# Attention with parallel feed-forward: shifted exponential readings summed in pairs by an accumulating DMA, and the normalisation on GpSimd

## The chip, the cores and the metric

One NeuronCore of one Trainium2 chip runs the whole program. The metric is the device time of one execution in microseconds (us). Each number for a kernel is the median of several executions.

## The reference

The kernel computes a layer norm of x (2048 rows of 640), multi-query attention with 32 heads of 20 columns and one shared key and value head, a feed-forward of 1728 columns with SiLU beside it, and the sum of both with x.

```
xn = layernorm(x)                                   # x: (1, 2048, 640) bf16
q  = (xn @ wq) as 32 heads of 20;  k = xn @ wk;  v = xn @ wv      # k, v: 2048 x 20
scores = q k^T / sqrt(20);  p = softmax(scores);  o = p v
out = x + (o as 2048 x 640) @ wo + silu(xn @ w1) @ w2
```

## The kernel before

**Blocks.** Scores are computed transposed, in blocks of 128 keys by 512 queries of one head: 32 heads x 4 query chunks x 16 key tiles = 2048 blocks (NB). Four heads of one query chunk form a group of 64 blocks (GB), so there are 32 groups (NG). A score step (do_S, matmuls at L1127) takes three or four blocks at once, each with a contraction of 20 rows in its own quarter of the array, into one PSUM bank per block.

**Two ways to an exponential.** Of a step's blocks, most are taken by ScalarE: one activation over two or three banks writes exp(scores) as bf16 into the ring E (L1161). The others (chosen in pick_dve) are taken by VectorE (L1176). The queries are scaled beforehand so that a score is in units of 1/128 of a power of two; adding OFF and writing the result as a 16-bit integer gives bits which, read as bf16, are a piecewise linear approximation of the exponential. This is a reading of the block, in a buffer Z that holds three blocks (a triple). To cancel the error of the approximation, GpSimd adds two constants to the bits (flush_z, L1202, as 64-bit integer adds over a whole triple), which gives two shifted readings in a buffer Y. The three readings of a block, with shifts 0, 43 and 86 and weights 1, 0.8046875 and 0.625 (PH), are all multiplied with V, and the three products are summed in PSUM. The weights are in V: self.v holds three copies of it, each scaled by its weight. A block of ScalarE uses copy 0 alone.

**PV.** The PV matmuls (do_pv, L968) take V as weights, 32 columns wide, four heads in the four quarters of the array, and accumulate over all keys in one PSUM bank per group. A 21st column of V holds half of the weight and gives the row sums of the softmax. A block of ScalarE is one such matmul, a block of VectorE is three.

**After a group** its bank is copied to U (L1245), transposed by a DMA issued on SP (L1216), and normalised on VectorE: a reciprocal of the sums (L1231) and one multiply (L1236), into o. When all heads of a query chunk are there, o is transposed by DMA (try_oT) and the output matmuls (out_job) follow.

**Other work on TensorE** is cut into jobs and laid between the score steps: the query projections (qd_job, whose results are copied to their places in qT by small DMAs on SP, L1303), the first feed-forward matmul (h_job, with a tanh on ScalarE, L1336, and a multiply on VectorE, L1341) and the second with the output projection (out_job, results at L1405, L1412, L1424).

**Order.** The order of every engine's instructions is made while the program is built. A planner (class Sched and Builder.step) runs a model of the five engines in which each instruction has a duration and a priority. It commits instructions one after the other, and the program is these five lists with semaphore waits between them, so on the chip no engine changes its order. The model's numbers (durations, the time after which a DMA's result counts as there, thresholds for choices) therefore set what stands behind what. 29 thresholds (28 before the change) are given anew for each 32 blocks, in a table SEG of 64 rows. Those that matter here: TILE_CAP is the number of VectorE blocks that a head may have (in self.nz), DVE_TH and DVE_TH2 the planned backlog of VectorE up to which a step gives it a first and a second block. NZ, NY and NBLK are the numbers of Z buffers, Y buffers and blocks in E.

Of the kernel before, what the change touches and what calls it, by code (L numbers as in the profile page):

```python
# [8 lines left out]
BF16 = mybir.dt.bfloat16  # L9
# [5 lines left out]
ALU = mybir.AluOpType  # L15

P = 128
# [18 lines left out]
UT_LATE = 2.0  # L36
UT_LATE1 = 4.0
# [8 lines left out]
PH = ((0, 1.0), (43, 0.8046875), (86, 0.625))  # L46
# [4 lines left out]
NBLK = 35  # L51
NZ = 8
NY = 4
# [51 lines left out]
YP_FIX = 0.147  # L105
YP_BLK = 0.218
# [13 lines left out]
            "ACT4", "SPLIT", "U2", "LOOK", "W4", "M3")  # L120
SEG = (
# [105 lines left out]
class Sched:  # L227
# [81 lines left out]
    def commit(self, op, start):  # L309
        e = op.eng  # L310
        if op.on_pick is not None:
            op.on_pick(op)
# [130 lines left out]
def t_dve_ps(n):  # L443
    return n / 960.0 + 0.067
# [1438 lines left out]
```

## Time and profile before

| | |
|---|---|
| median of 3 runs | 669.36 us (669.29 to 669.47) |
| profiled execution | 669.12 us, of which 667.3 us from the first to the last instruction (the span) |
| granted TensorE clock | 1.00 throughout |
| TensorE busy | 659.4 us |
| ScalarE busy | 647.7 us |
| VectorE busy | 601.3 us |
| GpSimd busy | 404.6 us |

The span has three parts. In the first 18.5 us the rows of x are loaded, their statistics taken and the first projections made. From 18.5 us, where the first exponential starts, to about 654 us ScalarE takes one exponential after the other while TensorE, VectorE and GpSimd work beside it. The last 13 us are the last group's normalisation and the last output matmuls. In the views below PE is TensorE's array, PEld its weight port, DVE VectorE, ACT ScalarE, POOL GpSimd and SP the engine that issues most DMAs; L with a number is a line of the kernel. Instructions that issue a DMA do not count as busy. A matmul's duration includes its way through the array, so the next begins before its end. A row of a wait names the engine and line that waited, what ended the wait, the total, the number of waits and the longest one.

### The profile page before, as it was taken

The page shows a single profiled execution, that of the slowest core. Times are in us where ns is not written, and L with a number is a line of the kernel's source. Part 1 is how long each engine was busy: PE and PEld are TensorE (multiplying, and loading weights), DVE is VectorE, ACT ScalarE, POOL GpSimd, SP SyncE. Part 2 cuts the span into 40 slices and gives each one's busy share as a digit, 9 for nine tenths or more (in the row PEclk, how much of TensorE's full clock was granted, in tenths as well). Part 3 has the DMA queues.
Part 4 walks back from the last instruction along what each step waited for, and adds up shares of the span by engine and source line. Part 5 has one row for each costly group of instructions (what it writes and reads, how often), then busy time and mean ns, then how long its engine had stood idle before and what let it go on. Part 6 is the DMA issues. An engine that isn't in the chain of part 4 may idle for free.

```text
span 667.3 us, 22800 instructions
## 1 busy us (share of the span) xinstructions
PE 659.4 (99%) x9735; PEld 220.4 (33%) x9735; DVE 601.3 (90%) x1085; ACT 647.7 (97%) x737; POOL 404.6 (61%) x509
## 2 busy tenths in 40 slices
PE   8999999999999999999999999999999999999998
PEld 4432233332323322233333323233233333223345
DVE  7888999999989999999889999988999999998783
ACT  7999999999999999999999999999999999999993
POOL 2056457777486656676556653866767674676550
PEclk9999999999999999999999999999999999999999
DMA  7565201010012210000003110000002121001001
GB/s 211 110 213 150 73 14 12 2 26 2 18 44 62 57 10 17 3 10 18 19 10 84 41 32 17 10 10 18 10 13 47 38 57 37 10 10 31 5 11 41
DMA packets 51433, 26.73 MB, mean 40 GB/s; under 512 B 38566, under 2 KB 50694, under 8 KB 51334
## 3 DMA queue, kind: packets, MB, share of 16 engines
q1 hardware_dynamic: 51190, 25.12, 14.5%
q8 instruction: 78, 1.28, 0.8%
q14 instruction: 21, 0.17, 0.1%
q10 hardware_dynamic: 144, 0.16, 0.1%
HBM read 11.44 MB, written 2.62 MB: 21 GB/s over the span
## 4 chain that ended last, share of the span: by engine, by line
PE 87%; ACT 7%; DVE 3%; SPq 1%; DMA 1%; issue 0%; ACTq 0%
PE psall L968 33%; PE psall L1127 28%; PE psall L870 26%; ACT sbt L1161 6%; DVE sbt L1176 2%; ACT sbt L1336 1%; SPq L1531 1%; DMA sbt<-in_A_x_dram 1%; DVE sbt L1424 0%; PE psall L1326 0%; DVE sbt L1236 0%; ACT sbt L1620 0%; DVE sbt L1666 0%; DVE sbt L1771 0%; ACT sbt L1655 0%
## 5 line engine op out<-in xcount | busy, mean ns | idle before, releaser
L1161 ACT ACTIVATE sbt<-psall 128x1024 bf16<-128x1024 f32 (+2 forms) x649 | 620.1, 1129 | 3.5 <-PE psall L1127 2.6
L1202 POOL INT64_ADD sbt<-sbt x492 | 399.7, 827 | 244.4 <-DVE sbt L1176 171.3
L1176 DVE TENSOR_SCALAR sbt<-psall 128x512 uint16<-128x512 f32 x732 | 473.1, 683 | 46.3 <-PE psall L1127 37.1
L968 PE MATMUL psall<-sbt 128*32 128x512 bf16 x3512 | 265.0, 383 | 0.2
L1127 PE MATMUL psall<-sbt 32*128 32x512 bf16 x2048 | 245.8, 384 | 2.1 <-ACT sbt L1161 0.7
L870 PE MATMUL psall<-sbt 128*32 128x320 bf16 (+2 forms) x3923 | 220.7, 331 | 0.5 <-DVE sbt L1176 0.4
L1127 PEld LDWEIGHTS psall<-sbt 32*128 32x128 bf16 x2048 | 61.9, 91 | 241.4 <-ACT sbt L1161 161.1
L870 PEld LDWEIGHTS psall<-sbt 128*32 128x32 bf16 x3923 | 84.6, 95 | 84.6 <-issue 54.4
L968 PEld LDWEIGHTS psall<-sbt 128*32 128x32 bf16 x3512 | 64.4, 95 | 101.3 <-issue 64.6
L1336 ACT ACTIVATE sbt<-psall 128x512 bf16<-128x512 f32 x54 | 39.6, 739 | 0.0
L1341 DVE SCALAR_TENSOR_TENSOR sbt<-sbt,psall 128x512 bf16<-128x512 bf16 x54 | 36.6, 682 | 2.6 <-ACT sbt L1336 1.2
L1245 DVE CAST sbt<-psall 128x512 bf16<-128x512 f32 x32 | 21.8, 681 | 5.4 <-PE psall L968 5.3
L1236 DVE TENSOR_TENSOR sbt<-sbt 128x320 bf16<-128x320 bf16 x31 | 18.3, 591 | 0.1
L846 PE MATMUL psall<-sbt 128*128 128x512 bf16 (+4 forms) x55 | 15.2, 428 | 1.2 <-DVE sbt L1590 1.2
L1424 DVE SCALAR_TENSOR_TENSOR sbt<-psall,sbt 128x320 bf16<-128x320 f32 x28 | 13.1, 477 | 2.9 <-PE psall L870 2.9
L1405 DVE SCALAR_TENSOR_TENSOR sbt<-psall,sbt 128x320 bf16<-128x320 f32 x28 | 13.5, 483 | 1.6 <-PE psall L870 1.4
L1294 DVE TENSOR_SCALAR sbt<-psall 128x512 bf16<-128x512 f32 (+1 forms) x19 | 12.9, 680 | 0.1
L1635 DVE BATCH_NORM_STATS2 sbt<-sbt 128x6 f32<-128x320 bf16 x22 | 10.0, 470 | 0.9 <-DMA sbt<-in_A_x_dram 0.7
L1421 ACT ACTIVATE sbt<-psall 128x320 bf16<-128x320 f32 x4 | 1.7, 438 | 8.7 <-PE psall L870 8.7
L846 PEld LDWEIGHTS psall<-sbt 128*128 128x128 bf16 x55 | 5.5, 109 | 9.1 <-issue 4.0
L1231 DVE RECIPROCAL sbt<-sbt 128x16 f32<-128x16 bf16 x31 | 7.5, 243 | 0.0
L1620 ACT ACTIVATE sbt<-sbt 128x640 bf16<-128x640 bf16 x5 | 3.6, 730 | 3.2 <-DMA sbt<-in_A_x_dram 3.2
(57 smaller groups left out, 70.1 us busy)
## 6 DMA issues: line engine op xcount, KB each, us to landing
sbt<-in_A_x_dram SPq DMA_DIRECT2D x32, 160.0 KB, 3.2
out_dram<-sbt SPq DMA_DIRECT2D x15, 160.0 KB, 2.0
sbt<-in_B_w_dram SPq DMA_DIRECT2D x5, 432.0 KB, 5.3
sbt<-sbt SPq DMA_DIRECT2D x105, 20.0 KB
sbt<-in_B_w_dram SPq DMA_DIRECT2D x13, 160.0 KB, 3.1
sbt<-sbt SPq DMA_TRANSPOSE x58, 2.5
sbt<-in_A_wo_dram SPq DMA_DIRECT2D x5, 160.0 KB, 3.1
sbt<-in_A_wq_dram SPq DMA_DIRECT2D x5, 140.0 KB, 3.1
```

Source lines behind the costliest of these rows:

```text
L846: return pe.matmul(self.bk(b, 0, n), self.zero[:, 0:P], self.zero[:, 0:n], start=True, stop=True)
L870: ins = pe.matmul(self.bk(b, 0, n, r, r + SLOT), w[:, r:r + SLOT], x, start=start, stop=stop, tile_position=(0, r), skip_group_check=True)
L968: ins = pe.matmul(self.bk(ub[k], 0, QW, r, r + SLOT), self.v[:, it.w, it.kt, :], it.x(), start=f, stop=False, tile_position=(0, r), skip_g ...
L1127: ins = pe.matmul(self.bk(bank[x]), self.kT[r:r + SLOT, kt * P:(kt + 1) * P], self.qT[r:r + SLOT, g % QS, :], start=True, stop=True, tile_ ...
L1161: return a.activation(self.E[:, b0 * QW:(b0 + na) * QW].rearrange("p (b n) -> p b n", n=QW), src, AF.Exp, scale=ACT_SCALE)
L1176: return v.tensor_scalar(self.Z[:, zs, zp * QW:(zp + 1) * QW], self.bk(bb), OFF, ZMAX, ALU.add, ALU.min)
L1202: sc.new("pool", YP_FIX + YP_BLK * n, lambda g, k=k: g.int64_add(self.Y[:, ys, k, 0:w].bitcast(I64), self.Z[:, zs, 0:w].bitcast(I64), PH[k ...
L1236: sc.new("dve", t_dve_ps(16 * DH), lambda v: v.tensor_tensor(dst, ut[:, :, :, 0:DH], rb, ALU.mult), [key, ("rL", up)], [("o", h0 + i) for ...
L1245: sc.new("dve", t_dve_ps(QW), lambda v: v.tensor_copy(self.U[:, up, :], self.bk(ub)), [("B", ub)], [("U", up)], prio=U_PRIO, name=f"Uev{g}")
L1336: sc.new("act", t_act(QW), lambda a: a.activation(t, src, AF.Tanh, scale=0.5), [("B", b)], [("tb", tp)], prio=TH_PRIO, name=f"th{c}_{fk}") ...
L1341: sc.new("dve", t_dve_ps(QW), lambda v: v.scalar_tensor_tensor(out=self.hT[0:rows, fk, :], in0=t, scalar=1.0, in1=src, op0=ALU.add, op1=AL ...
L1405: sc.new("dve", t_dve_ps(320), lambda v: v.scalar_tensor_tensor(out=in1, in0=ps, scalar=0.5, in1=in1, op0=ALU.mult, op1=ALU.add), [("B", b ...
```

## The change

The two shifted readings get one common weight: shifts 39 and 82, weight 0.71875 for both, so V is kept in two copies. Because of that, the two readings of a triple may be added before the matmul. For many triples GpSimd issues a DMA, behind the two integer adds, that adds the second reading to the first in SBUF, as bf16 (accum_op add; 128 partitions of 3072 bytes). Such a triple has one more reading for PV and not two. A triple is merged when it is full (three blocks), the planned backlog of GpSimd is under MG, the planned time is past 78 us, and at least 16 blocks of its group are still to come. A merged block counts as half a block in self.nz.

The multiply that normalises a group's U moves from VectorE to GpSimd, except for the last group. The reciprocal stays on VectorE.

The planner gets durations for this: 0.9 us for the issue, a summed reading that is there 5.7 us after the issue starts or later, GpSimd's next three instructions behind an issue longer by 0.28, 0.22 and 0.12 us, 1.0 us for the normalisation on GpSimd; results of the U transposes and of the small q copies that it counts as there 1.8 us later than before. There are six Z buffers in place of eight, five Y buffers in place of four, and 36 blocks of E in place of 35.

The table SEG has new rows throughout, with MG as a 29th column (0 to 4, mean 2.4). The mean of DVE_TH over the 64 rows goes from 5.85 to 7.57, of DVE_TH2 from 1.87 to 2.00, of TILE_CAP from 7.14 to 7.16.

```
-UT_LATE = 2.0
-UT_LATE1 = 4.0
+UT_LATE = 3.8
+UT_LATE1 = 5.0
...
-PH = ((0, 1.0), (43, 0.8046875), (86, 0.625))
+SHIFT = (39, 82)
+VW = (1.0, 0.71875)
+NRM = 1.0
+NRM_PRIO = 3.0
+ACC_ISSUE = 0.9
+ACC_LAND = 5.7
+ACC_RATE = 165e3
+ACC_NEXT = (0.28, 0.22, 0.12)
+ACC_FROM = 78.0
+ACC_DMA = 1.8
+MG = 3.0
+MG_END = 16
...
-NBLK = 35
-NZ = 8
-NY = 4
+NBLK = 36
+NZ = 6
+NY = 5
...
-YP_FIX = 0.147
-YP_BLK = 0.218
+YP_FIX = 0.159
+YP_BLK = 0.222
...
# SEG: 64 rows replaced, one column (MG) added
...
# Sched.commit
+        if e == "pool":
+            if op.dma:
+                self.after_acc = 0
+            else:
+                if self.after_acc < len(ACC_NEXT):
+                    op.dur += ACC_NEXT[self.after_acc]
+                self.after_acc += 1
...
-                op.avail = max(op.end + 2.0, q + op.mode / 375e3) + op.late
+                op.avail = max(op.end + 2.0, q + op.mode / (ACC_RATE if op.name == "acc" else 375e3)) + op.late
...
-        self.v = sb([P, 3, KT, SLOT], BF16)
+        self.v = sb([P, 2, KT, SLOT], BF16)
...
# flush_z
+        g1 = self.zblocks[-1][1]
+        back = max(sc.t["pool"] - sc.t["pe"], 0.0) + sum(o.dur for o in sc.pend["pool"])
+        merge = n == ZB and back < MG and sc.t["pe"] > ACC_FROM and self.bp < GB * (g1 + 1) - MG_END
...
-                PH[k + 1][0] * 0x0001000100010001), zk + [("lib",)], [("Y", ys, k, i) for i in range(n)],
+                SHIFT[k] * 0x0001000100010001), zk + [("lib",)], [("Y", ys, k, i) for i in range(n)],
...
+        if merge:
+            op = sc.dma("pool", lambda g: g.dma_start(
+                self.Y[:, ys, 0, 0:w].bitcast(BF16), self.Y[:, ys, 1, 0:w].bitcast(BF16), accum_op=ALU.add),
+                [("Y", ys, 1, i) for i in range(n)], [("Y", ys, 0, i) for i in range(n)], P * w * 2,
+                sem=self.acc_sem[ys], prio=3.9, name="acc")
+            op.dur = ACC_ISSUE
+            op.late = ACC_LAND - 2.0 - ACC_ISSUE
+            self.acc_no[ys] += 1
+            op.inc_no = self.acc_no[ys]
+            self.merged += 1
+            for _, g, kt, j in self.zblocks:
+                self.nz[g][j] -= 0.5
         for i, (t, g, kt, j) in enumerate(self.zblocks):
-            for k in range(2):
-                self.item(g, j, kt, k + 1, lambda k=k, i=i: self.Y[:, ys, k, i * QW:(i + 1) * QW].bitcast(BF16),
-                          [("Y", ys, k, i)])
+            for k in range(1 if merge else 2):
+                self.item(g, j, kt, 1,
+                          lambda k=k, i=i: self.Y[:, ys, k, i * QW:(i + 1) * QW].bitcast(BF16), [("Y", ys, k, i)])
...
# normalise
-        sc.new("dve", t_dve_ps(16 * DH), lambda v: v.tensor_tensor(
+        pool = g < self.NG - 1
+        sc.new("pool" if pool else "dve", NRM if pool else t_dve_ps(16 * DH), lambda v: v.tensor_tensor(
             dst, ut[:, :, :, 0:DH], rb, ALU.mult), [key, ("rL", up)], [("o", h0 + i) for i in range(4)],
-            prio=U_PRIO if g < self.NG - 1 else -1.0, name=f"nrm{g}")
+            prio=NRM_PRIO if pool else -1.0, name=f"nrm{g}")
...
# qd_job: the small copies of q
+                ops[-1].late = ACC_DMA if sc.t["pe"] > ACC_FROM else 0.0
...
# prologue: one memset and one scaled copy of V less
-        for k in range(3):
-            pool(0.15, lambda g, k=k: g.memset(self.v[:, k, :, DH:DH + 1], 0.5 * PH[k][1]), [("v0",)],
+        for k in range(2):
+            pool(0.15, lambda g, k=k: g.memset(self.v[:, k, :, DH:DH + 1], 0.5 * VW[k]), [("v0",)],
...
-                for k in range(3):
+                for k in range(2):
...
-                        self.v[:, k, n0:n1, 0:DH], sv, PH[k][1], None, ALU.mult),
+                        self.v[:, k, n0:n1, 0:DH], sv, VW[k], None, ALU.mult),
```

More of the change, by code (lines that the diff above doesn't have):

```diff
@@ L119 @@
             "ZWAIT", "Y0_POOL", "Y0_COST", "JOB_BURST", "TILE_CAP", "E_HIGH", "Q_LEAD", "U_GO", "U_Z", "JU_E", "STRETCH",
-            "ACT4", "SPLIT", "U2", "LOOK", "W4", "M3")
+            "ACT4", "SPLIT", "U2", "LOOK", "W4", "M3", "MG")
 SEG = (
[64 rows of a table removed]
[64 rows of a table added]
 )
@@ L244, in __init__ @@
         self.dmaq = defaultdict(float)
+        self.after_acc = 99
     def sem(self, name):
@@ L594, in steps_init @@
         self.yset = 0
+        self.merged = 0
+        self.acc_no = [0] * NY
+        self.acc_sem = [self.sc.sem(f"acc{i}") for i in range(NY)]
         self.zblocks = []
```

128 rows, old and new, of the table SEG are left out of this document.

## The prediction

> **What bounds the kernel now.** I read the busy times on the page first, then the chain that ended last, then the busy times by stretch, then the groups, the waits, and last the timeline of a few microseconds in the middle.
>
> ```profile
> PE 659.4 (99%) x9735; PEld 220.4 (33%) x9735; DVE 601.3 (90%) x1085; ACT 647.7 (97%) x737; POOL 404.6 (61%) x509
> PE 87%; ACT 7%; DVE 3%; SPq 1%; DMA 1%; issue 0%; ACTq 0%
> ```
>
> ```profile
> core 0: us, PE busy (x) PEld busy (x) DVE busy (x) ACT busy (x) POOL busy (x), PEclk, DMA share, GB/s
> 0.00:80.00 80.00, 76.25 (x896) 28.29 (x896) 68.62 (x185) 74.71 (x100) 30.51 (x50) 1.00 0.55 157
> 80.00:640.00 560.00, 558.90 (x8333) 179.02 (x8328) 518.98 (x874) 557.71 (x621) 367.42 (x452) 1.00 0.10 24
> 640.00:667.30 27.30, 24.24 (x525) 13.12 (x513) 13.74 (x28) 15.27 (x20) 6.64 (x8) 1.00 0.08 26
> ```
>
> From 80 to 640 us TensorE is busy for 558.9 and ScalarE for 557.7 of 560 us. VectorE follows with 519.0 (93%). GpSimd is idle for 193 us of them and the DMA engines for 90%.
>
> ```profile
> L1161 ACT ACTIVATE sbt<-psall 128x1024 bf16<-128x1024 f32 (+2 forms) x649 | 620.1, 1129 | 3.5 <-PE psall L1127 2.6
> L1202 POOL INT64_ADD sbt<-sbt x492 | 399.7, 827 | 244.4 <-DVE sbt L1176 171.3
> L1176 DVE TENSOR_SCALAR sbt<-psall 128x512 uint16<-128x512 f32 x732 | 473.1, 683 | 46.3 <-PE psall L1127 37.1
> L968 PE MATMUL psall<-sbt 128*32 128x512 bf16 x3512 | 265.0, 383 | 0.2
> L1236 DVE TENSOR_TENSOR sbt<-sbt 128x320 bf16<-128x320 bf16 x31 | 18.3, 591 | 0.1
> ```
>
> Of 2048 score blocks 732 take their exponential on VectorE and 1316 on ScalarE. A ScalarE block costs one PV matmul, a VectorE block three: 1316 + 3 x 732 = 3512, which is the count at L968. So the choice of engine trades ScalarE time against VectorE and TensorE time. A busy TensorE could still be a waiting one, so its rate is read from the timeline:
>
> ```profile
> 299.78 8.40 ACT L1161 ACTIVATE sbt<-psall 128x1024 bf16<-128x1024 f32 x9
> 308.46 0.40 PE L968 MATMUL psall<-sbt 128*32 128x512 bf16 x4
> 308.80 0.39 PE L1127 MATMUL psall<-sbt 32*128 32x512 bf16 x3
> 309.01 3.21 DVE L1176 TENSOR_SCALAR sbt<-psall 128x512 uint16<-128x512 f32 x5
> 309.12 0.83 PE L968 MATMUL psall<-sbt 128*32 128x512 bf16 x12
> 309.88 0.10 PEld L1127 LDWEIGHTS psall<-sbt 32*128 32x128 bf16 x4 [0.42 <-ACT sbt L1161]
> ```
>
> Twelve PV matmuls (three passes of four) take 0.83 us and four take 0.40, so a pass more costs 0.22 us, a matmul 0.055. The three passes from 309.12 are through at about 309.78, and the score matmuls start at 309.88: the 0.10 us between is what stands at every change of kind (308.80 to 309.12 is a pass and 0.11). The 0.42 us "waited for ACT" before them is time of the weight port, not lost array time. Both engines are thus full, and a shorter span needs less work on both. The marginal prices: 8.40 / 18 = 0.467 us of ScalarE a block, 3.21 / 5 = 0.642 us of VectorE.
>
> **The change: what a merge saves.** A merged triple's two shifted readings become one, so its three blocks need six PV matmuls and not nine: 3 x 0.055 = 0.165 us of TensorE. Alone that buys nothing, since ScalarE stays full. TensorE time must be turned into more VectorE blocks, each of which takes 0.467 us from ScalarE and gives TensorE 2 x 0.055 = 0.11 us. The planner's rules open that way: a merged block counts as half against the cap per head, and the mean backlog threshold DVE_TH over the 64 rows rises from 5.85 to 7.57. With m merges and d moved blocks both engines get shorter alike when 0.467 d = 0.165 m - 0.11 d, so d = 0.286 m and the gain is 0.133 m.
>
> **How many merges.** Merging starts at 78 us and is left out in a group's last 16 of 64 blocks. From 80 us there are 452 / 2 = 226 triples, so at most 0.75 x 226 = 170 can be merged. The other limit is GpSimd, because a triple is merged only while its planned backlog is below MG (0 to 4 us).
>
> ```profile
> L1202 POOL INT64_ADD sbt<-sbt x492: 394/827/1054, 32.5 to 650.2; - x164
> L1236 DVE TENSOR_TENSOR sbt<-sbt x31: 471/483/1072, 60.8 to 640.3; 128x320 bf16<-128x320 bf16 x31
> L1428 SPq DMA_DIRECT2D out_dram<-sbt x15: 332/427/578, 204.9 to 664.8; - x15
> L1216 SPq DMA_TRANSPOSE sbt<-sbt x31: 1189/1209/1976, 55.3 to 636.2; - x31
> ```
>
> Held at 90% of 560 us, GpSimd has 504 - 367 = 137 us to give. The 31 normalisations take some: no row has one on GpSimd, and VectorE's rows bound it between 0.48 and 1.07; I take 0.8, in the middle, 25 us. The eight triples more of the result below take 8 x 2 x 0.827 = 13 us. There remain 99 us. What the issue of an accumulating DMA costs GpSimd no row shows: the DMA issues on SP lie between 0.33 us (a plain output) and 1.98 (the longest transpose). I take 1.2, the median transpose, because it too moves SBUF to SBUF in many pieces. That makes m = 82, with 50 and 170 (the cap) at the ends.
>
> [...]
>
> **What VectorE allows.** The normalisation leaves it with 601.3 - 18.3 = 583.0 us. At m = 82, d = 23, it has 583.0 + 15 = 598 us in a span of 656, 91%; TensorE saves 13.5 - 2.6 = 10.9 us and ScalarE 10.9. If VectorE can be held no fuller than now (90.1%), then 583.0 + 0.642 d = 0.901 x (667.3 - 0.467 d), d = 17, and the gain is 8.0 us. Both limits are near; I take the middle, 9.5 us.
>
> **What costs nothing, and under which cover.** The normalisation waits on GpSimd for the transposed U and for VectorE's reciprocal; queued behind it are the next integer adds, and their readers are PV matmuls. The cover is how long readings lie ready:
>
> ```profile
> POOL sbt L1202 <- DVE sbt L1176: 171.3, 178, 27.1
> POOL sbt L1202 <- PE psall L968: 69.5, 16, 10.4
> PEld psall L968 <- issue: 64.6, 285, 0.2
> PEld psall L968 <- POOL sbt L1202: 15.9, 69, 0.3
> ```
>
> GpSimd spent 69.5 us in 16 waits for PV matmuls to free its output buffers, up to 10.4 us at once, so readings usually wait for TensorE. PV matmuls waited for GpSimd 69 times at 0.23 us each, which is what 285 changes of kind cost without any wait (64.6 / 285 = 0.23): lost time there is about nil. If this cover were gone, each microsecond of GpSimd's delay would be one of TensorE's. The fifth Y set, the two fewer Z sets and E's 36th block only move where buffers come free; between nothing and a few of those 69.5 us, off the path. Two V copies instead of three drop a third of a memset and four small evictions:
>
> ```profile
> L1597 POOL MEMSET sbt<- 128x1536 bf16 x1 | 1.4, 1379 | 0.0
> L1804 DVE TENSOR_SCALAR sbt<-psall 128x80 bf16<-128x80 f32 x12 | 2.8, 233 | 0.1
> ```
>
> That is 0.5 us of GpSimd before its first add at 32.5 us and 0.9 us of VectorE. PV is not late in the prologue, so I take nothing, with 0.9 us as the other end.
>
> **The landing.** The planner puts a summed reading's PV matmul at the earliest 5.7 us after GpSimd starts the issue (0.9 + 2.0 + 2.8). A triple is 384 KB.
>
> ```profile
> sbt<-in_A_x_dram SPq DMA_DIRECT2D x32, 160.0 KB, 3.2
> sbt<-in_B_w_dram SPq DMA_DIRECT2D x5, 432.0 KB, 5.3
> sbt<-sbt SPq DMA_DIRECT2D x1, 512.0 KB, 3.7
> DMA to landing us min/median/max: 2.3/2.4/4.1
> ```
>
> The first two rows give 3.2 + 224 x 2.1 / 272 = 4.9 us for 384 KB, and the row inside SBUF gives less, 3.7 for 512 KB. If the destination's read counts like a second transfer, 768 KB come to 7.9 us by the same line. I take 4.9, between the two rows that resemble it, below the 5.7. The last row is the U transposes' (L1216): they share the DMA engines, and the planner now sets them 1.8 us later. The small q copies get 1.8 us too and are issued 54 steps ahead.
>
> [...]
>
> **The rivals.** (1) Slower: the sum lands late. TensorE runs its list in order, so a PV matmul whose summed reading has not landed holds all behind it, and ScalarE, whose next scores lie behind it, soon after. At the 7.9 us bound a sum is 2.2 us late. If a quarter of 82 merges are read at their earliest place, that is 20 x 2.2 = 44 us, and 704; at 1 us late, 20 us and 680. It decides from 9.5 / 82 = 0.12 us of mean wait per merge. For it speaks that no row shows an accumulating DMA; against it the waits above. (2) GpSimd fills early: at 1.98 us an issue m is 50, the gain 6.7; if slow issues also push adds back, less, 664 to 668. For it speaks its 66% already. (3) More merges than I think: m of 120 to 170 gives 16 to 22 us, 647 to 653; against it, VectorE would have to stand at 95% (d = 48: 614 of 645 us). (4) The change doesn't do what it says: few triples pass the tests or ScalarE's share stays, and the time stays at 669. Against it stands the half count.
>
> **How the numbers follow.** The profiled execution took 669.1 us, 1.8 beyond its span of 667.3; the median of the runs is 669.36. 669.36 - 9.5 = 659.9 us. The forecast's own range, with gains from 5.5 to 16, is 653 to 664. About 0.2% is what a measurement of this kernel can tell from no change. Chances: forecast 0.49, (3) 0.12, (2) 0.11, (4) 0.05, and (1) 0.23, of which some 0.1 lies above 678. So faster has 0.72, no change 0.05, slower 0.23. For 8 in 10 the range reaches down into (3), to 647, and up into the mild part of (1), to 678.
>
> **What would show it.** In the changed profile: L968's matmuls number 2048 + 2 x (VectorE blocks) - 3 m, which gives m, expected near 82 and between 50 and 120; VectorE's exponentials rise from 732 to about 755 and ScalarE's time at its exponentials falls by some 11 us; the normalisations stand on GpSimd, whose busy time, in which DMA issues do not count, grows from 404.6 to about 443 us; VectorE is at 90 to 92%. A step is wrong if PV matmuls wait for the accumulating DMA or for GpSimd by more than the 0.23 us of a change of kind, or if ScalarE, full from 80 to 640 us now, shows gaps that end with score matmuls. The prediction fails if those waits add up to over 9 us, or if the exponentials on VectorE don't rise.

## The result, and the profile after

The changed kernel takes 1045.18 us (1044.46 to 1045.83, 4 runs) where the kernel before takes 669.33: a ratio of 1.562, 95% interval 1.559 to 1.564. The forecast was 659.9 and the range 647 to 678; the forecast, the range and the sign are all wrong. The profiled execution took 1045.32 us, its span 1043.5, and the granted TensorE clock averaged 0.825 where it had been 1.00.

The busy times of the page after, and the chain that ended last:

```profile
PE 721.2 (69%) x9484; PEld 219.8 (21%) x9487; DVE 598.6 (57%) x1058; ACT 656.5 (63%) x738; POOL 509.2 (49%) x635
PE 53%; issue 21%; POOL 9%; ACT 7%; DVE 6%; DMA 3%; SPq 0%; POOLq 0%; ACTq 0%
```

The engines do about the work they did, but no engine is full any more: ScalarE's 656 us now lie in 1043. "issue", in which an engine waits for nothing that the profile shows, has 21% of the chain, from 0%. The groups say where:

```profile
L1183 ACT ACTIVATE sbt<-psall 128x1024 bf16<-128x1024 f32 (+1 forms) x650 | 625.4, 1069 | 371.6 <-PE psall L1149 368.6
L1227 POOL INT64_ADD sbt<-sbt x502 | 424.5, 930 | 284.9 <-issue 165.9
L990 PE MATMUL psall<-sbt 128*32 128x512 bf16 x3270 | 291.2, 431 | 308.6 <-POOL sbt L1227 293.8
L1274 POOL TENSOR_TENSOR sbt<-sbt 128x320 bf16<-128x320 bf16 x31 | 22.3, 718 | 222.3 <-issue 115.7
L1232 POOL DMA_DIRECT2D sbt<-sbt x86 | 86.5, 1006 | 11.2 <-POOL sbt L1227 11.1
```

Read from the bottom: 86 triples are merged, and GpSimd's idle time ahead of those DMAs is 11 us. Ahead of the 31 normalising multiplies it is 222.3 us, 7.2 each. TensorE's PV matmuls (L990) wait 294 us for GpSimd's integer adds, and ScalarE 369 us for TensorE. What is issued at GpSimd's two lines besides the instructions themselves:

```profile
L1274 POOLq MODIFY_POOL_CONFIG  x62: 1/21/794, 55.2 to 1006.5; - x62
L1227 POOLq MODIFY_POOL_CONFIG  x62: 1/1/318, 64.2 to 1015.0; - x62
```

The kernel before has none at these two lines, only a pair in its prologue, at load_lib (L1579). Here there are four per multiply, two at its own line and two at the next add's. One place in order of time, picked from the timeline:

```profile
412.06 0.39 PE L1149 MATMUL psall<-sbt 32*128 32x512 bf16 x3
413.47 0.72 POOL L1274 TENSOR_TENSOR sbt<-sbt 128x320 bf16<-128x320 bf16 x1 [7.18 <-DVE sbt L1198]
420.30 6.43 POOL L1227 INT64_ADD sbt<-sbt  x8 [6.12 <-issue]
421.18 0.62 PE L990 MATMUL psall<-sbt 128*32 128x512 bf16 x4 [8.72 <-POOL sbt L1227]
421.98 1.04 PE L990 MATMUL psall<-sbt 128*32 128x512 bf16 x8 [0.19 <-POOL sbt L1227]
423.62 1.02 ACT L1183 ACTIVATE sbt<-psall 128x1024 bf16<-128x1024 f32 x1 [9.89 <-PE psall L1149]
424.91 0.62 PE L990 MATMUL psall<-sbt 128*32 128x512 bf16 x8
```

GpSimd stands still for 7.2 us, multiplies for 0.72, stands still for 6.1 us and then works through eight adds that had piled up. TensorE ran out of readings at 412.45 and waits 8.7 us; ScalarE 9.9. When TensorE resumes, eight matmuls take 1.04 us, and from 424.91 on 0.62 as before: it comes back slowly for about 3.7 us. The granted clock (the first number behind the five busy times) says why:

```profile
412.40:415.00 2.60, 0.05 (x3) 0.00 (x0) 0.85 (x2) 1.33 (x2) 0.72 (x1) 0.91 0.03 6
415.00:421.18 6.18, 0.01 (x2) 0.01 (x2) 0.00 (x0) 0.00 (x0) 0.88 (x2) 0.50 0.00 0
421.18:424.91 3.73, 3.54 (x28) 0.66 (x28) 1.29 (x2) 1.02 (x1) 3.73 (x5) 0.52 0.00 0
424.91:427.00 2.09, 2.09 (x34) 0.66 (x35) 1.61 (x3) 1.97 (x3) 2.09 (x4) 1.00 0.00 0
```

It is half from about 414.5 (0.91 over the first row's 2.60 us) to about 424.75 (0.52 over the third row's 3.73 us). So here it fell about 2 us after the end of the last matmul (412.45) and rose about 3.6 us after the matmuls resumed (421.18). These are the times of this one place; what sets them was not tried.

### The profile page after: what moved, and what is told of

Read it like the earlier page. It is cut to its first block, busy times and chain, and to the rows that moved or that the text cites. A ratio compares the mean times of both kernels' runs of the same rounds, so it can differ in the third digit from the quotient of the medians.

```text
span 1043.5 us, 22556 instructions
## 1 busy us (share of the span) xinstructions
PE 721.2 (69%) x9484; PEld 219.8 (21%) x9487; DVE 598.6 (57%) x1058; ACT 656.5 (63%) x738; POOL 509.2 (49%) x635
## 2 busy tenths in 40 slices
DMA packets 63817, 60.54 MB, mean 58 GB/s; under 512 B 39942, under 2 KB 52070, under 8 KB 63718
## 4 chain that ended last, share of the span: by engine, by line
PE 53%; issue 21%; POOL 9%; ACT 7%; DVE 6%; DMA 3%; SPq 0%; POOLq 0%; ACTq 0%
PE psall L990 20%; PE psall L1149 18%; PE psall L892 15%; POOL sbt L1227 6%; ACT sbt L1183 5%; DVE sbt L1198 5%; DMA sbt<-sbt 3%; POOL sbt L1274 2%; POOL sbt L1232 1%; ACT sbt L1375 1%; DMA sbt<-in_A_x_dram 0%; SPq L1570 0%; DVE sbt L1380 0%; ACT sbt L1659 0%; PE psall L1818 0%
## 5 line engine op out<-in xcount | busy, mean ns | idle before, releaser
L1183 ACT ACTIVATE sbt<-psall 128x1024 bf16<-128x1024 f32 (+1 forms) x650 | 625.4, 1069 | 371.6 <-PE psall L1149 368.6
L1198 DVE TENSOR_SCALAR sbt<-psall 128x512 uint16<-128x512 f32 x740 | 485.4, 686 | 414.6 <-PE psall L1149 406.9
L1227 POOL INT64_ADD sbt<-sbt x502 | 424.5, 930 | 284.9 <-issue 165.9
L990 PE MATMUL psall<-sbt 128*32 128x512 bf16 x3270 | 291.2, 431 | 308.6 <-POOL sbt L1227 293.8
L1149 PE MATMUL psall<-sbt 32*128 32x512 bf16 x2048 | 268.7, 415 | 3.3 <-DVE sbt L1451 1.2
L892 PE MATMUL psall<-sbt 128*32 128x320 bf16 (+2 forms) x3923 | 236.0, 344 | 0.4 <-DVE sbt L1380 0.2
L990 PEld LDWEIGHTS psall<-sbt 128*32 128x32 bf16 x3270 | 63.1, 97 | 430.0 <-POOL sbt L1227 323.0
L1274 POOL TENSOR_TENSOR sbt<-sbt 128x320 bf16<-128x320 bf16 x31 | 22.3, 718 | 222.3 <-issue 115.7
L1232 POOL DMA_DIRECT2D sbt<-sbt x86 | 86.5, 1006 | 11.2 <-POOL sbt L1227 11.1
L1375 ACT ACTIVATE sbt<-psall 128x512 bf16<-128x512 f32 x54 | 36.6, 678 | 0.0
L868 PE MATMUL psall<-sbt 128*128 128x512 bf16 (+4 forms) x46 | 12.4, 417 | 1.5 <-DVE sbt L1629 1.2
```

What stands on the lines that cost most here:

```text
L868: return pe.matmul(self.bk(b, 0, n), self.zero[:, 0:P], self.zero[:, 0:n], start=True, stop=True)
L892: ins = pe.matmul(self.bk(b, 0, n, r, r + SLOT), w[:, r:r + SLOT], x, start=start, stop=stop, tile_position=(0, r), skip_group_check=True)
L990: ins = pe.matmul(self.bk(ub[k], 0, QW, r, r + SLOT), self.v[:, it.w, it.kt, :], it.x(), start=f, stop=False, tile_position=(0, r), skip_g ...
L1149: ins = pe.matmul(self.bk(bank[x]), self.kT[r:r + SLOT, kt * P:(kt + 1) * P], self.qT[r:r + SLOT, g % QS, :], start=True, stop=True, tile_ ...
L1183: return a.activation(self.E[:, b0 * QW:(b0 + na) * QW].rearrange("p (b n) -> p b n", n=QW), src, AF.Exp, scale=ACT_SCALE)
L1198: return v.tensor_scalar(self.Z[:, zs, zp * QW:(zp + 1) * QW], self.bk(bb), OFF, ZMAX, ALU.add, ALU.min)
```

## The experiments

**The theories.** Code loads: each multiply between integer adds costs a standstill of GpSimd before it and one after it, 7.2 and 6.1 us at the place above. That GpSimd loads another program in them is my guess, and no trace shows it; what the runs can test is whether the standstills come with the multiply. Late sums: the accumulating DMA lands too late (the rival of the prediction). Held list: the multiply's wait for the U transpose and the reciprocal holds the adds behind it.

**The multiply back on VectorE.** In normalise:

```
-        pool = g < self.NG - 1
+        pool = False
...
-            prio=NRM_PRIO if pool else -1.0, name=f"nrm{g}")
+            prio=U_PRIO if g < self.NG - 1 else -1.0, name=f"nrm{g}")
```

> The changed kernel with the normalising multiply back on VectorE; merging and all else stay. Code loads (GpSimd reloads its program for every multiply and again for the next integer add, 31 x 13 us): the 62 loads are gone, VectorE gets 18 us back, and the time falls from 1045 to between 655 and 672, at a granted clock of 1.00. Late sums (the accumulating DMA holds TensorE): merging is still there, so at least 1000. Held list (the multiply's wait for the U transpose and the reciprocal holds GpSimd's adds): the wait is gone from GpSimd, so 655 to 672 as well; this run doesn't tell it from code loads.

701.78 us, ratio 1.049 (1.047 to 1.051), with 110 merges. The MODIFY_POOL_CONFIG rows at the adds are gone. So 343 of the 376 us belong to where the multiply stands, and late sums as the main cause, which asked for at least 1000, are out. But 702 is 30 us above the 672 that the other two theories allowed. Where those come from is taken up below.

**The multiply on GpSimd alone**, in the kernel before:

```
-        sc.new("dve", t_dve_ps(16 * DH), lambda v: v.tensor_tensor(
+        pool = g < self.NG - 1
+        sc.new("pool" if pool else "dve", 1.0 if pool else t_dve_ps(16 * DH), lambda v: v.tensor_tensor(
...
+            prio=3.0 if pool else -1.0, name=f"nrm{g}")
```

> The kernel before with the normalising multiply on GpSimd and nothing else changed: no merging, three copies of V. Code loads: 62 loads of 6 to 7 us, most of them shown in the span: 1000 to 1080. Late sums: no summed reading is left, so 665 to 672. Held list: 1000 to 1080 too.

1007.18 us, ratio 1.504: without any merging the slowdown is nearly whole. Late sums predicted 665 to 672.

**One element instead of 320**, and **a memset instead of a multiply**, each as one more instruction per group in the kernel before:

```
+            sc.new("pool", 0.15, lambda v: v.tensor_tensor(self.pj[:, :], rl[:, 0, 0:1], rl[:, 0, 1:2], ALU.mult),
+                   [("rL", up)], [("pj",)], prio=3.0, name=f"pj{g}")
...
# the second kernel has v.memset(self.pj[:, :], 0.0) there, with the same wait
```

> The kernel before, normalising on VectorE as it was, with one more instruction on GpSimd per group: a multiply of one element per partition, behind the reciprocal, whose result nobody reads. Code loads: the size does not matter, 31 x 12 us: 1000 to 1080, with MODIFY_POOL_CONFIG rows in the profile. Held list: the wait for the reciprocal holds the adds as in the changed kernel, 900 to 1080. If the length of the multiply itself or its reading beside VectorE mattered: 669 to 675. Late sums: 669.

> As the run with the tiny multiply, but the instruction is a memset of one element per partition behind the same reciprocal, in the same place of the plan. Code loads: a memset ran between two adds in the kernel before without a gap of 6 us, so 669 to 676. Held list: the same wait at the same place, so as long as the tiny multiply, 900 to 1080. Late sums: 669.

970.56 us with the multiply (ratio 1.450), 669.49 with the memset (0.9999, 0.9989 to 1.0009). The rows on the line of the tiny multiply, then all that stands on the memset's:

```profile
L1241 POOLq MODIFY_POOL_CONFIG  x62: 1/11/13, 60.1 to 932.7; - x62
L1241 POOL TENSOR_TENSOR sbt<-sbt x31: 183/184/188, 67.2 to 939.6; 128x1 f32<-128x1 f32 x31
```

```profile
L1241 POOL MEMSET sbt<- x31: 97/98/100, 60.5 to 639.9; 128x1 f32 x31
```

An instruction of 0.18 us costs 301 / 31 = 9.7 us; one with the same wait at the same place costs nothing. The held list falls, and little of the price is the multiply's length: 9.7 us each at 0.18 us, (1007.18 - 669.62) / 31 = 10.9 at 0.72 us in the run with the whole multiply. It is the kind of instruction. (Both multiplies have two inputs, the memset none, and the copy of the next run one; whether it is the multiply or its second input is not told apart.) The adds behind the multiplies waited 165.9 us in 28 cases for "issue" in the changed kernel, 5.9 each; the multiplies waited 7.2. That a program is fetched in these gaps is not seen here: the DMA engines moved 60.54 MB in the changed kernel and 60.53 in the last run below, which has no multiply on GpSimd. What the runs show is the standstill, with MODIFY_POOL_CONFIG rows in front of it.

**The changed kernel without the standstills.** Every list stays as it is, only the multiply becomes a copy, so the normalisation is left out:

```
+        ... lambda v: v.tensor_copy(dst, ut[:, :, :, 0:DH]) if pool else v.tensor_tensor(
```

> The changed kernel with every instruction list as it is; only the 31 multiplies on GpSimd become copies of U of the same shape, at the same places and behind the same waits (normalisation is left out of this run). Code loads: a copy needs no other program on GpSimd, so the 62 loads go and what is left is the change as it was meant: 655 to 667, clock 1.00, 86 merges. Late sums: as the run with the multiply on VectorE under a new plan took 702, the sums or the issues cost 30 us there; if they do so here, 685 to 710. If the copy too needs a load: 1000 to 1050.

664.49 us, ratio 0.992 (0.991 to 0.994). Its page, the same stretch of GpSimd, and the groups:

```profile
PE 651.1 (98%) x9484; PEld 214.6 (32%) x9487; DVE 592.7 (89%) x1058; ACT 643.0 (97%) x738; POOL 494.7 (75%) x635
```

```profile
406.80 0.83 POOL L1227 INT64_ADD sbt<-sbt  x1 [1.57 <-DVE sbt L1198]
407.57 0.45 POOL L1274 COPY sbt<-sbt 128x320 bf16<-128x320 bf16 x1
408.00 0.82 POOL L1227 INT64_ADD sbt<-sbt  x1
```

```profile
L1183 ACT ACTIVATE sbt<-psall 128x1024 bf16<-128x1024 f32 (+1 forms) x650 | 617.6, 1148 | 4.9 <-PE psall L1149 2.7
L1227 POOL INT64_ADD sbt<-sbt x502 | 425.5, 902 | 127.0 <-DVE sbt L1198 114.8
L1198 DVE TENSOR_SCALAR sbt<-psall 128x512 uint16<-128x512 f32 x740 | 480.2, 684 | 42.7 <-PE psall L1149 32.1
L1232 POOL DMA_DIRECT2D sbt<-sbt x86 | 79.0, 918 | 11.1 <-POOL sbt L1227 11.0
L1274 POOL COPY sbt<-sbt 128x320 bf16<-128x320 bf16 x31 | 14.9, 480 | 12.8 <-DVE sbt L1268 12.7
```

The copy stands between two adds with no gap. Between this run and the changed kernel the instructions of TensorE, VectorE and ScalarE are the same, so their difference of 380.7 us of span is what the multiplies' standstills cost: TensorE busy 721.2 against 651.1, 70 us more at a granted clock of 0.825 against 1.00, and idle 322.3 against 11.7, 311 us. The 31 pairs of gaps make 31 x (7.2 + 5.9) = 406 us; the span grew by 94% of that. Two small things lie in these sums besides: 12.8 us of the gaps ahead stand in the copy run too, as waits for the reciprocal, and the multiply takes 0.72 us where the copy takes 0.48.

**Half of the multiplies.** In the run below the changed lists are kept, and multiplies are moved to VectorE's list at their planned start; here only those of the even groups:

> As the run before, but only the multiplies of the even groups move to VectorE; the 15 of odd groups stay on GpSimd. Code loads: 30 loads and not 62, so about half way from that run to the 1045 us of the changed kernel: 830 to 870. If it were one disturbance for the whole run (a lower clock, a first load): near 1045, or near the run without any.

850.74 us. The 15 multiplies left on GpSimd cost (850.74 - 664.49) / 15 = 12.4 us each, all 31 cost (1045.18 - 664.49) / 31 = 12.3: the price goes with the number of multiplies there. (The even groups' multiplies on VectorE add a little, see below.)

**The lists kept, all multiplies on VectorE.** They are taken out of GpSimd's list after planning:

```
+        for op in move:                       # the multiplies, before emit
+            self.order["pool"].remove(op)
+            op.eng = "dve"
+            i = next((i for i, o in enumerate(self.order["dve"]) if o.start > op.start), len(self.order["dve"]))
+            self.order["dve"].insert(i, op)
```

> The changed kernel with its lists kept, but each multiply taken out of GpSimd's list and put into VectorE's at the place that fits its planned start; everything is computed. If the 702 us of the first run came from the new plan that the planner made for it: 658 to 672 here (the multiplies cost VectorE 15 to 27 us, of which its free time hides most). Late sums, or GpSimd slowing VectorE's multiplies: 685 to 710.

678.38 us, ratio 1.014 (1.012 to 1.015): between the two expectations. Of the 702 us of the first run 23 therefore came from the new plan that was made once the planner knew the multiply to be on VectorE. It merges 110 triples where the kept plan merges 86; which of its differences costs the 23 us was not tried. 14 us over the copy run remain. The multiplies' group, their shortest, median and longest in ns, and one of them beside GpSimd:

```profile
L1286 DVE TENSOR_TENSOR sbt<-sbt 128x320 bf16<-128x320 bf16 x31 | 25.4, 820 | 0.0
L1286 DVE TENSOR_TENSOR sbt<-sbt x31: 471/572/2680, 56.5 to 648.6; 128x320 bf16<-128x320 bf16 x31
```

```profile
319.71 3.53 POOL L1239 INT64_ADD sbt<-sbt  x4
```

```profile
321.31 2.28 DVE L1286 TENSOR_TENSOR sbt<-sbt 128x320 bf16<-128x320 bf16 x1
```

It lasts until GpSimd's four adds are over (323.24) and 0.35 us more. The trace has 18 multiplies that start while an add is running, and each ends 0.34 to 0.36 us behind the end of an add, after 0.52 to 2.68 us; the other 13 take 0.47 to 0.48. In the kernel before the group had 18.3 us, 0.59 each. Either this or the mere 15 us (31 x 0.48) that even short multiplies put on VectorE could be the 14 us.

**One input in SBUF.** The multiply is replaced by an instruction with one SBUF input at the same place, in two runs:

```
# first:  v.reciprocal(dst, ut[:, :, :, 0:DH])
# second: v.bn_stats(self.st6[:, 0, 0, :], the first 320 columns of UT)
```

> As the run that kept the plan and moved the multiplies to VectorE (678 us), but each of the 31 is a reciprocal of the same 128x320 elements, with one input in SBUF and not two (normalisation is left out of this run). If the 14 us over the copy run come from VectorE and GpSimd both wanting SBUF for a two-input multiply (it took up to 2.7 us there, 0.47 at the least): its longest goes back to about its shortest, and the time to 664 to 670. If they come from the 0.5 us that each takes from VectorE at a place where none was planned: 676 to 680, with longest and shortest alike.

725.75 us, and no verdict: the reciprocal was the wrong stand-in.

```profile
L1278 DVE RECIPROCAL sbt<-sbt 128x320 bf16<-128x320 bf16 x31 | 66.4, 2142 | 0.0
L1278 DVE RECIPROCAL sbt<-sbt x31: 2131/2143/2147, 56.2 to 699.7; 128x320 bf16<-128x320 bf16 x31
```

It is long everywhere and adds 61 us, so the time says nothing. But its shortest and longest lie 16 ns apart, though 18 of the 31 start while an add is running: writing 320 columns to SBUF beside the adds lengthened nothing here.

> The run before failed to tell the two apart: its reciprocal took 2.14 us at every place, so length was added (61 us for 31 x 2.14 = 66 us of VectorE, 0.92 us for each). Here each of the 31 is a statistics instruction over 320 elements of U, one input in SBUF, which took 0.47 us in the prologue (normalisation is left out of this run). If VectorE's time at unplanned places is what costs: 31 x 0.47 x 0.92 = 13 us over the copy run, 676 to 680, as the multiplies did with 25 us of VectorE in all. If two inputs in SBUF beside GpSimd are the cost: lengths all near 0.47 and 664 to 671.

666.76 us, ratio 0.996 (0.995 to 0.997).

```profile
L1286 DVE BATCH_NORM_STATS2 sbt<-sbt x31: 474/484/489, 56.5 to 637.4; 128x6 f32<-128x320 bf16 x31
```

All 31 take 0.48 us at the same places, again with 18 of them starting beside an add, and cost 2.3 us of span together. So time of VectorE at these places is nearly free, and the 0.92 us for each microsecond, worked out from the long reciprocals, does not hold for short ones. What cost 12 of the 14 us is the multiply beside GpSimd's adds: 0.48 us alone, up to 2.68 beside them, where the two one-input instructions kept their length within 16 ns. That it is the second SBUF input, and not another difference between these instructions, is my reading of these three and was not tried alone. The trace also has a multiply that waited out as many as three adds in a row, not only the one that was running.

**A version from this.** The multiplies stay on VectorE, each is put where GpSimd's list has its gap, and GpSimd's next instruction waits for it:

```
+            # in the loop above: a, b = neighbours in GpSimd's list, s = start of a VectorE instruction in their gap
+            op.start = at - 1e-4
+            nxt.deps.add(op)                  # nxt = b
```

> The kernel with the changed plan and the multiplies on VectorE (678 us), everything computed, with one thing more: each multiply is placed where GpSimd's list has its gap, and GpSimd's next instruction waits for it, so that no add runs beside it. If an add beside a multiply is what makes it long: the multiplies' mean falls from 0.82 to about 0.5 us and the time to 665 to 670, near the 667 of the one-input run. If the multiply then only waits for the add in front: mean over 0.7 and 672 to 679.

666.94 us (665.82 to 667.57, 6 runs), ratio 0.996 (0.995 to 0.998): everything is computed, and it is 0.4% faster than the kernel before.

```profile
L1309 DVE TENSOR_TENSOR sbt<-sbt 128x320 bf16<-128x320 bf16 x31 | 14.9, 482 | 0.0
```

## Why the prediction was wrong

**The step that failed** is the price of the normalisation on GpSimd, "no row has one on GpSimd, and VectorE's rows bound it between 0.48 and 1.07; I take 0.8". The multiply itself took 0.72 us, inside the bounds. What was missing is that GpSimd stands still at each change between the multiply and the adds: 13.1 us for each multiply, sixteen times the term, of which 12.3 reached the time. The bounds came from another engine; the trace of before has no such operation on GpSimd, and the 13.1 us that it paid in the changed kernel beside the multiply's 0.72 stood in no row of VectorE. That trace held a hint: after the first adds GpSimd ran nothing but integer adds and a memset, and the prologue loads a library for the add (load_lib), with its one pair of MODIFY_POOL_CONFIG rows.

**The cover** was read rightly. It was said that without it each microsecond of GpSimd's delay would be one of TensorE's: 406 us of gaps became 381 of span. The prediction's own sign of failure, waits of PV matmuls for GpSimd of over 9 us in all, came: 294 us at L990. The 69.5 us of waits for free buffers that I counted as cover are spread over 16 waits of up to 10.4 us; 13 us at a time, 31 times, is more than they hold.

**Rival (1)** had the sign but not the cause. The sums landed 4.2 us after their issue (median; 3.8 to 6.0 in the copy run, 4.9 estimated, 5.7 allowed for). In the copy run TensorE waited for none of them; in the changed kernel six waits for a DMA make 17 us.

**The rest of the sum** is seen in the copy run. Merges: 82 expected, 86 measured, and 2048 + 2 x 740 - 3 x 86 = 3270 is the count at L990. The issue: 1.2 us taken, 0.92 measured; the adds rose from 0.83 to 0.90 on average. GpSimd's busy time came to 495 us, since the page does count the issues there, 79 us that lie partly beside adds; without them the trace has 442 us (adds 425.5, copies 14.9, memsets), where 443 were expected. The gain was 5.0 us (669.45 - 664.49, both measured together) where 9.5 were expected, and the term that was mis-sized is the number of moved blocks: 8 (732 to 740), not 17 to 23. Eight blocks are 8 x 0.467 = 3.7 us of ScalarE, whose busy time fell by 4.7. The 14 us (86 x 0.165) that merging took from TensorE did not become blocks; ScalarE stayed full, as the text said it would if blocks did not move, and VectorE at 89% had room. That the plan, not the chip, kept them on ScalarE is argued from this and was not tried.

## What to carry to other kernels

Before work is moved to an engine, look whether the trace shows that engine running this kind of instruction between the neighbours it will have; where it does not, put one tiny instruction of that kind there and measure it, since here the bounds from another engine's rows missed the 13.1 us that GpSimd paid for each multiply between its adds. When a list is made by a planner with thresholds fitted to it, test one step with the lists held fixed: taking one step back and planning anew mixed 23 us of a new plan into the first answer here. And a stand-in for an instruction must have its length as well as its operands, or it answers another question.

## What the runs showed of the hardware that was not expected

- A tensor_tensor on GpSimd between integer adds: a standstill of 7.2 us before it and 5.9 us behind it at 320 elements, 12.3 us of span each; with one element 9.7 us of span each. A copy of 320 elements (0.45 us) and a memset (0.10 us) at the same place have none.
- A two-input multiply on VectorE, 0.48 us alone, took up to 2.68 us beside GpSimd's adds and ended 0.34 to 0.36 us behind the end of an add; a one-input instruction of the same size took 0.474 to 0.489 in all 31 cases.
- A reciprocal on VectorE took 2.14 us for 128 x 320 bf16, 4.4 times the multiply of the same shape.
- An accumulating DMA of 384 KB inside SBUF, issued from GpSimd, occupied GpSimd for 0.92 us in the copy run (1.01 in the changed kernel) and landed in 4.2 us in both, faster than the 4.9 us that the loads of 160 and 432 KB suggested.
